# Attention and two feed-forward layers on one core: three experts' weights split straight into their place

## The chip, the cores and the metric

One Trainium2 chip, of which the kernel uses one core. The metric is device time in microseconds (us) of one execution. The engines are named as in the profile: PE is TensorE's matmul and PEld its weight load, DVE is VectorE, ACT is ScalarE, POOL is GpSimd, SP is SyncE, which issues nearly all transfers. POOL issues the gathers and the scattered stores of rows.

## The reference

```python
def _attn_ref(q, k, v, i_gate, f_gate, o_gate):      # B=4, H=8, S=768, D=40
    for t in range(S):
        m_new = np.maximum(f_gate[:, :, t] + m, i_gate[:, :, t])
        ...
        C = f_stab[:, :, None, None] * C + i_stab[:, :, None, None] * np.einsum('bhd,bhe->bhde', vt, kt)
        n = f_stab[:, :, None] * n + i_stab[:, :, None] * kt
        y[:, :, t] = o * h_tilde / denom

def _moe_ref(x, w_in, w_out, alpha):                 # 3072 tokens, 320 -> 2048 -> 320
    h = x @ w_in
    g = np.maximum(h, 0.0) + alpha * np.minimum(h, 0.0)
    return (g @ w_out).astype(np.float32)

def _moe2_ref(x, w_gate, w_output_gate, w1, w2):     # 8 experts, 320 -> 1024 -> 320
    e_idx = np.argmax(x @ w_gate, axis=1)
    ...
    for e in range(E):
        mask = e_idx == e
        h = np.maximum(x[mask] @ w1[e], 0.0)
        out[mask] = gate_w[mask, None] * eom[mask, e, None] * (h @ w2[e])
```

A gated recurrent attention feeds a dense layer, whose result picks one of eight experts for each token. Every expert's two matrices are needed, and which token goes to which expert is known only when the dense layer is through.

## The kernel before

**Stages.** The attention runs in 24 units of 128 positions (4 batches of 6). Three units make a block of 384 tokens, so the dense layer has 8 blocks. In a block it goes through the 2048 inner columns in 16 chunks of 128: `ffn1` (code F) makes a chunk in 8 matmuls, `ffn_split` (g) splits it into a rounded part and a remainder, `ffn2` (S) adds it into the block's output in 9 matmuls. `block_out` and `block_out2` (bo, bp) take a block's output, choose the expert of every token and store the rows to `x1d` in memory. Behind the last block the tokens are sorted by expert (`route_a` to `route_d`, `route_bh`), and 28 to 32 slots of 128 tokens, each of one expert, go through that expert's matrices: slot 0 by `first_rows`, `first_x`, `first_1`, `first_t`, `first_2`, the others in the loop `slots`.

**Split numbers.** A product in nearly full precision is made of products of two rounded parts, so a weight matrix is needed as a high part and a remainder (hi and lo): an ACT copy rounds, and DVE or POOL subtracts. The dense layer's weights come as 64-bit words and are put together on DVE first (`dec_wi`, `dec_wo`).

**The ring.** `ring` is one tile of 33,792 columns, place for the hi and lo parts of three experts (11,264 columns each, RC). While the dense layer runs, the same columns hold its own split weights (16 chunks of wi and wo), the split q and k of the attention (qh, kh), the transposed input of a block (xt_even, xt_odd), the split chunks (gsp) and a pair of tiles for splitting (ehs). They are handed out in that order by `carve`.

**The experts' weights.** Each expert's matrices are cut into 8 pieces (four of 768 columns, four of 640), so there are 64. All through the dense layer a piece is loaded into a staging tile (`expert_load`, el), split (`expert_split`, es: ACT copy, then POOL or DVE) and stored, hi and lo, to a scratch area `scr` in memory (`expert_store`, et). In the last block, as the columns of `ring` come free from the left, `early_load` (ld) reads the first three experts back from `scr` in 33 loads of 1024 columns. The experts behind them are loaded in the slot loop by `next_load`, when the place of one that is done comes free.

**What sets the order.** One list, ORDER, holds the codes of all steps in the order in which they are written out; the table OTHER says for each step whether it takes its usual engine or the other one. Each engine runs its own instructions strictly in that order. The staging tiles (tag raw) are three; the 64-bit words, the experts' pieces and, in `route_c`, the table `a1` share them. `warm` is a matmul on a part of `ring` that was set to zero; its result isn't used.

The split of an expert's piece before (lines 1097 and 1098 of the profile):

```python
A.activation(eh[:, :n], st[:, :n], AF.Copy)
engine(G, V, "expert_split", x).tensor_tensor(st[:, :n].bitcast(F32R), st[:, :n], eh[:, :n].bitcast(F32), ALU.subtract)
```

Other lines that are spoken of: L837 F's matmuls, L845 and L846 the two steps of its activation (ACT, DVE), L852 and L853 its split (ACT, DVE), L865 to L868 S's matmuls, L642 and L650 the products with the gate columns (`gate_w`, `gate_w2`: pw, pwg), L714 the scores of the attention (ps), L971 `route_bh`, L1043 `a1`, L1055 its product (ptok), L331 the gathers of a slot's rows (xg), L1154 `warm`.

## Time and profile before

| | |
|---|---|
| three timed executions, us | 806.36, 809.18, 810.07 (median 809.18) |
| the profiled execution, us | 803.76 |
| its span, first to last instruction, us | 801.7 |
| mean granted TensorE clock, share of full | 0.971 |
| busy: PE, DVE, ACT, POOL | 96%, 58%, 50%, 31% of the span |

The time of an execution holds about 2 us that lie outside the span. The profile's rows come from the one profiled execution, which was shorter than the three timed ones. Busy times of one engine's neighbours overlap a little, since an instruction starts before the one ahead has wholly left the engine.

### The profile page before, as it was taken

How to read it: one execution, taken by the hardware profiler on the slowest of the kernel's cores; microseconds unless marked ns; L12 is line 12 of the kernel's file. 1: busy time of each engine (PE TensorE's matmuls, PEld its weight loads, DVE VectorE, ACT ScalarE, POOL GpSimd, SP SyncE). 2: the span in 40 equal slices, each digit the busy share in tenths (PEclk: the TensorE clock that was granted, in tenths of full speed). 3: DMA queues.
4: the chain of work that ended last, by engine and by line, in shares of the span. 5: the costliest groups of instructions: out<-in, count | busy, mean ns of one | idle time of the engine just before them, and what ended most of it. 6: DMA issues, size and time to landing. Idle time of an engine off the chain costs nothing.

```text
span 801.7 us, 15145 instructions
## 1 busy us (share of the span) xinstructions
PE 766.3 (96%) x4823; PEld 728.3 (91%) x4823; DVE 468.6 (58%) x1143; ACT 400.3 (50%) x846; POOL 252.0 (31%) x266
## 2 busy tenths in 40 slices
PE   3999999999999999999999999986999999999995
PEld 2888999999999999999999999985799999989994
DVE  6757999777666777666677766855323223223231
ACT  3624667647766578567467574332323333233231
POOL 1311323231655443536234432112223222222221
PEclk9857999999999999999999999999999999999998
DMA  7835678988899989998999888989746744661000
GB/s 226 254 130 165 221 244 247 278 252 275 249 306 315 304 285 284 279 285 310 291 292 278 297 271 274 327 295 301 260 169 227 298 161 179 266 249 43 31 20 13
DMA packets 84272, 189.45 MB, mean 236 GB/s; under 512 B 8786, under 2 KB 39567, under 8 KB 82914
## 3 DMA queue, kind: packets, MB, share of 16 engines
q1 hardware_dynamic: 80802, 179.74, 68.8%
q0 software_dynamic: 3392, 8.71, 3.2%
q8 instruction: 44, 0.72, 0.4%
q14 instruction: 34, 0.28, 0.1%
HBM read 267.71 MB, written 55.59 MB: 403 GB/s over the span
## 4 chain that ended last, share of the span: by engine, by line
PE 85%; DMA 6%; issue 3%; ACT 3%; DVE 2%; POOL 1%; POOLq 0%; SPq 0%; ACTq 0%; DVEq 0%
PE ph L837 20%; PE p L293 12%; PE po L293 11%; PE acc L865 7%; PE acc L866 6%; PE acc L868 6%; PE pa L781 5%; PE ps L714 4%; PE p L375 3%; PE pb L730 2%; PE pd L753 2%; PE pwg L650 2%; PE warm L1154 2%; DMA scr<-ring 1%; PE xt L341 1%
## 5 line engine op out<-in xcount | busy, mean ns | idle before, releaser
L837 PE MATMUL ph<-ring 128*128 128x384 f32 x1024 | 198.8, 342 | 0.4 <-DVE ring L853 0.3
L837 PEld LDWEIGHTS ph<-ring 128*128 128x128 f32 x1024 | 176.6, 188 | 2.4 <-DVE ring L853 1.9
L865 PE MATMUL acc<-ring 128*128 128x336 f32 x384 | 123.4, 327 | 0.7 <-ACT ring L852 0.4
L866 PE MATMUL acc<-ring 128*128 128x336 f32 x384 | 120.0, 318 | 0.0
L846 DVE SCALAR_TENSOR_TENSOR ph<-v,al,ph 128x384 f32<-128x384 f32 x128 | 78.1, 618 | 53.9 <-ACT v L845 53.1
L845 ACT ACTIVATE v<-ph 128x384 f32<-128x384 f32 x128 | 61.7, 488 | 80.4 <-PE ph L837 80.2
L293 PE MATMUL po<-ring,hh 128*128 (+1 forms) x448 | 99.3, 308 | 1.0 <-DMA ring<-scr 1.0
L397 DVE TENSOR_SCALAR yo<-po,xg 128x320 f32<-128x320 f32 x27 | 14.9, 551 | 143.9 <-PE po L293 143.9
L293 PE MATMUL p<-ring,xh 128*128 (+1 forms) x336 | 94.4, 402 | 0.6 <-ACT xh L344 0.6
L1098 POOL TENSOR_TENSOR er<-er,ring 128x768 fp32r<-128x768 f32 (+1 forms) x38 | 65.9, 1739 | 82.1 <-ACT ring L1097 81.9
L853 DVE TENSOR_TENSOR ring<-ph,ring 128x384 fp32r<-128x384 f32 x128 | 70.6, 554 | 25.9 <-ACT ring L852 23.0
L852 ACT ACTIVATE ring<-ph 128x384 fp32r<-128x384 f32 x128 | 62.0, 488 | 40.6 <-DVE ph L846 35.7
L398 POOL DMA_INDIRECT out_dram<-yo,tok x28 | 28.4, 1016 | 169.3 <-DVE yo L397 161.5
L868 PE MATMUL acc<-ring 128*128 128x336 f32 x384 | 80.4, 318 | 0.0
L293 PEld LDWEIGHTS po<-ring,hh 128*128 128x128 f32 x448 | 75.8, 187 | 3.9 <-ACT hr L364 1.4
L378 ACT ACTIVATE hh<-p 128x512 fp32r<-128x512 f32 x56 | 30.6, 598 | 93.4 <-PE p L375 93.4
L865 PEld LDWEIGHTS acc<-ring 128*128 128x128 f32 x384 | 73.0, 190 | 1.6 <-ACT ring L852 0.7
L293 PEld LDWEIGHTS p<-ring,xh 128*128 128x128 f32 x336 | 61.6, 190 | 13.2 <-ACT xh L344 0.8
L866 PEld LDWEIGHTS acc<-ring 128*128 128x128 f32 x384 | 72.7, 189 | 0.1
L293 PE MATMUL po<-ring,hl 128*128 (+1 forms) x224 | 69.0, 308 | 0.2 <-DVE hl L379 0.2
L364 ACT ACTIVATE hr<-p 128x512 f32<-128x512 f32 x56 | 33.4, 597 | 69.8 <-PE p L293 69.8
L868 PEld LDWEIGHTS acc<-ring 128*128 128x128 f32 x384 | 64.0, 190 | 0.0
(193 smaller groups left out, 1275.4 us busy)
## 6 DMA issues: line engine op xcount, KB each, us to landing
ring<-scr SPq DMA_DIRECT2D x28, 3072.0 KB
ring<-scr SPq DMA_DIRECT2D x28, 2560.0 KB
ring<-scr SPq DMA_DIRECT2D x33, 512.0 KB
D<-gd SPq DMA_DIRECT2D x48, 256.0 KB
er<-in_ew_dram SPq DMA_DIRECT2D x32, 384.0 KB
scr<-ring SPq DMA_DIRECT2D x32, 384.0 KB
scr<-er SPq DMA_DIRECT2D x32, 384.0 KB
er<-in_ew_dram SPq DMA_DIRECT2D x32, 320.0 KB
```

The source lines that it names most:

```text
L293: mm = T.matmul(o_, lhsT, r, start=start, stop=stop)
L364: A.activation(hr[:, hf * 512 : (hf + 1) * 512], ph, AF.Relu)
L781: T.matmul(pa[:, h * 41 : (h + 1) * 41], t["D", h // 4][:, h % 4], v1[:, h * 41 : (h + 1) * 41], start=True, stop=True,)
L837: T.matmul(ph[:, :384], wi_[i][lo][:, wc], xTs[n % 2][:, xc], start=(a == 0), stop=(a == len(PASSES) - 1),)
L845: A.activation(v, ph[:, :384], AF.Relu, scale=-1.0)
L846: V.scalar_tensor_tensor(ph[:, :384], v, al1[:, i : i + 1], ph[:, :384], ALU.mult, ALU.add)
L852: A.activation(gh, v, AF.Copy)
L853: V.tensor_tensor(gl, v, gh.bitcast(F32), ALU.subtract)
L865: T.matmul(ac, gh[:, sl], hi, start=(i == 0), stop=False)
L866: T.matmul(ac, gh[:, sl], lo, start=False, stop=False)
L868: T.matmul(accs[n][t][:, :NO], gl[:, t * P : (t + 1) * P], hi, start=False, stop=(i == NFC - 1))
L1098: engine(G, V, "expert_split", x).tensor_tensor(st[:, :n].bitcast(F32R), st[:, :n], eh[:, :n].bitcast(F32), ALU.subtract)
```

## The change

The first three experts (24 of the 64 pieces) no longer go through the scratch area. `expert_load`, `expert_split` and `expert_store` run for the other 40 pieces alone, and `early_load` is gone. In its place `held_load` (hl) loads such a piece from the input into a staging tile, and `held_split` (hs) writes its two parts straight into their columns of `ring`: an ACT copy (hi) and a subtraction that always runs on DVE (lo). Three of the loads are issued ahead, the others between the steps of the last block and of slot 0. In `ring` qh now lies ahead of the last chunk of wi, and kh and xt_even near the end. ORDER and OTHER are new as a whole, and `warm` is there 13 times instead of 32.

```diff
-FIRST = 1024
+HELD = 3
...
     "expert_split": (
-        2, 3, 4, 6, 7, 9, 16, 19, 21, 22, 25, 26, 27, 29, 31, 36, 37, 38, 41, 44, 48, 52, 53, 57, 61,
-        63,
+        2, 3, 4, 6, 7, 9, 16, 19, 21, 22, 25, 26, 28, 29, 31, 33, 38, 40, 42, 45, 48, 53, 54, 57, 58,
+        59, 62, 63,
     ),
...
-    "warm": ("warm", zip(range(32))),
-    "el": ("expert_load", zip(range(64))),
+    "warm": ("warm", zip(range(13))),
+    "el": ("expert_load", zip(range(HELD * NPIECE, E * NPIECE))),
...
-    "ld": ("early_load", zip(range(33))),
+    "hl": ("held_load", zip(range(HELD * NPIECE))),
+    "hs": ("held_split", zip(range(HELD * NPIECE))),
...
-    def early_load(p_):
-        c0, c1 = p_ * FIRST, (p_ + 1) * FIRST
...
-            nc.sync.dma_start(ring[:, c0:c].bitcast(F32), scr[e, :, c0 - e * RC : c - e * RC])
...
-        qh = carve(H, P, rows=KR)
-        kh = carve(H, P, rows=KR)
-        xt_even = carve(5, 384)
         wi_, wo_ = [], []
-        for _ in range(NFC):
+        for i in range(NFC):
+            if i == NFC - 1:
+                qh = carve(H, P, rows=KR)
             wi_.append((carve(3, P), carve(3, P)))
...
         gsp = [(carve(384), carve(384)) for _ in range(3)]
+        kh = carve(H, P, rows=KR)
+        xt_even = carve(5, 384)
         ehs = [carve(PC) for _ in range(2)]
...
+        def held_load(x):
...
+            st = stp.tile([P, RW], F32, tag="raw", bufs=3, name=f"eh_{x}")
+            nc.sync.dma_start(st[:, :n], ew[e, :, c0 : c0 + n])
...
+        def held_split(x):
...
+            o = e * RC + base
+            hi, lo = ring[:, o : o + n], ring[:, o + half : o + half + n]
+            A.activation(hi, st, AF.Copy)
+            engine(V, G, "held_split", x).tensor_tensor(lo, st, hi.bitcast(F32), ALU.subtract)
```

In the diff's code V is DVE, G POOL and A ACT; held_split has no entry in OTHER, so its second step takes the usual engine, V. Lines behind the ones that are gone have moved up by 8 (L837 is now L829), those behind the new functions down by 10.

Three places of the new order. First PE in the first third of the start, where the attention of units 1 and 2 and the gate products wait for their inputs. Before:

```order
L781 MATMUL pa_408<-kv_1_208,D_1_325 128x41 x4
L822 MATMUL pt_424<-cst,y_389 128x128 x3
L1154 MATMUL warm_436<-ring 128x512
L1154 MATMUL warm_438<-ring 128x512
L1154 MATMUL warm_440<-ring 128x512
L1154 MATMUL warm_442<-ring 128x512
L650 MATMUL pwg_455<-wgt,woT_237 128x16 x3
L642 MATMUL pw_461<-cst,f_wo_343 128x128 x3
L1154 MATMUL warm_472<-ring 128x512
L1154 MATMUL warm_474<-ring 128x512
L714 MATMUL ps_0_483<-q_2_433,k_2_431 128x128 x4
```

The same place now:

```order
L773 MATMUL pa_414<-kv_1_317,D_1_271 128x41 x4
L634 MATMUL pw_433<-cst,f_wo_335 128x128 x3
L814 MATMUL pt_439<-cst,y_403 128x128 x3
L706 MATMUL ps_0_452<-q_2_358,k_2_446 128x128 x4
L1164 MATMUL warm_458<-ring 128x512
L706 MATMUL ps_1_474<-q_2_358,k_2_446 128x128 x4
```

Between the second half of unit 1's product with v (pa) and unit 2's scores (ps) six warm matmuls and one gate product (pwg) are gone. Counted up to the first F, PE's row holds 31 warm matmuls before and 13 now, 9 and 8 pw, 8 and 6 pwg, and the same steps of units 0 to 2.

Second ACT at the end of the last block, around the split of its chunks 14 and 15 (ph is a chunk, v its activation, xr a row tile of the block's output). Before:

```order
L852 ACTIVATE ring<-ph_6145 128x384
L344 ACTIVATE xh_6178<-xt_6174 128x384
L845 ACTIVATE v_6193<-ph_6184 128x384
L852 ACTIVATE ring<-ph_6184 128x384
L880 ACTIVATE xr_0_6218<-acc_0_5791 128x320
```

Now:

```order
L1092 ACTIVATE ring<-eh_5988 128x640
L844 ACTIVATE ring<-ph_5954 128x384
L837 ACTIVATE v_6033<-ph_6024 128x384
L1092 ACTIVATE ring<-eh_5994 128x640
L844 ACTIVATE ring<-ph_6024 128x384
L1092 ACTIVATE ring<-eh_6049 128x640
L1092 ACTIVATE ring<-eh_6053 128x640
L872 ACTIVATE xr_0_6076<-acc_0_5600 128x320
```

The copy of piece 13 (eh_5994) now stands ahead of the split of the last chunk (ph_6024); it writes columns of chunk 14, so it waits for that chunk's S. Slot 0's xh, which stood ahead of the last chunk, comes later.

Third DVE behind the last block, from the reciprocals of `block_out2` (xr) to the ranks of `route_c` (rb). Before:

```order
L912 TENSOR_TENSOR sm_6252<-sm_6252,zs_6256 128x3
L914 RECIPROCAL xr_0_6218<-sm_6252 128x4
L914 RECIPROCAL xr_1_6222<-sm_6252 128x4
L914 RECIPROCAL xr_2_6226<-sm_6252 128x4
L1025 TENSOR_TENSOR rb<-ranks,oh_all 128x24
```

Now:

```order
L906 RECIPROCAL xr_2_6084<-sm_6099 128x4
L1093 TENSOR_TENSOR ring<-eh_6060,ring 128x768
L1093 TENSOR_TENSOR ring<-eh_6062,ring 128x768
L336 TENSOR_TENSOR xl_6124<-xt_6119,xh_6123 128x256
L337 TENSOR_TENSOR xh_6123<-xt_6119,xh_6123 64x128
L1093 TENSOR_TENSOR ring<-eh_6073,ring 128x768
L1017 TENSOR_TENSOR rb<-ranks,oh_all 128x24
```

Three held pieces and slot 0's remainders now stand ahead of `route_c`. Behind `a1` two more pieces stand ahead of the token lists, and three more behind slot 0's splits; `route_d` follows these, ahead of slot 1's remainders.

## Rows read from the trace of the kernel before

**Rows 1.** The page: part 1 (busy time of each engine, its share of the span, instructions) and, of part 2, the granted clock of TensorE in 40 slices of 20 us.

```profile
PE 766.3 (96%) x4823; PEld 728.3 (91%) x4823; DVE 468.6 (58%) x1143; ACT 400.3 (50%) x846; POOL 252.0 (31%) x266
...
PEclk9857999999999999999999999999999999999998
```

**Rows 2.** Busy time by stretches of the span: us of the stretch, then for each engine busy us and (x) instructions, the granted clock, the DMA share and GB/s.

```profile
0.00:20.00 20.00, 6.77 (x25) 4.87 (x25) 12.66 (x39) 6.30 (x14) 2.16 (x7) 1.00 0.74 226
20.00:60.00 40.00, 39.03 (x170) 34.16 (x169) 27.34 (x70) 18.18 (x45) 10.90 (x14) 0.69 0.62 193
...
100.00:200.00 100.00, 99.91 (x682) 98.10 (x682) 80.72 (x191) 62.11 (x135) 29.59 (x34) 0.98 0.83 259
...
400.00:500.00 100.00, 99.31 (x651) 97.69 (x650) 71.00 (x171) 63.98 (x133) 40.10 (x38) 1.00 0.88 282
500.00:540.00 40.00, 37.85 (x251) 37.44 (x250) 26.87 (x79) 14.04 (x30) 5.32 (x10) 1.00 0.92 317
540.00:560.00 20.00, 14.93 (x100) 12.63 (x98) 11.14 (x57) 5.00 (x11) 4.15 (x8) 0.91 0.86 284
560.00:580.00 20.00, 17.59 (x97) 14.90 (x98) 6.37 (x14) 6.69 (x13) 4.95 (x5) 1.00 0.76 285
```

**Rows 3.** The same view in stretches of 4 us, around the first product of the dense layer.

```profile
36.00:40.00 4.00, 4.00 (x18) 3.51 (x18) 2.77 (x6) 0.84 (x1) 1.98 (x3) 0.50 0.87 263
...
64.00:68.00 4.00, 4.00 (x15) 3.19 (x15) 2.69 (x9) 1.41 (x3) 0.00 (x0) 0.50 0.40 129
68.00:72.00 4.00, 4.00 (x28) 3.43 (x26) 2.59 (x10) 2.54 (x7) 0.24 (x1) 0.79 0.79 242
72.00:76.00 4.00, 4.00 (x23) 3.45 (x23) 3.92 (x12) 2.74 (x9) 1.39 (x2) 1.00 0.87 263
```

**Rows 4.** The timeline of PE, in order of time, at the start: start us, us, engine, line, operation, out<-in, count, and in brackets the idle time before it and what ended it.

```profile
22.61 3.78 PE L714 MATMUL ps<-q,k 40*128 40x128 f32 x16
...
33.70 2.11 PE L714 MATMUL ps<-q,k 40*128 40x128 f32 x16
...
41.77 2.05 PE L1154 MATMUL warm<-ring 128*128 128x512 f32 x4
43.63 1.29 PE L650 MATMUL pwg<-wgt,woT 128*128 128x16 f32 x6
44.76 0.88 PE L642 MATMUL pw<-cst,f_wo 128*128 128x128 f32 x3
...
73.73 3.05 PE L837 MATMUL ph<-ring 128*128 128x384 f32 x16
...
105.18 1.41 PE L650 MATMUL pwg<-wgt,woT 128*128 128x16 f32 x12
```

**Rows 5.** Groups of instructions by line with their shapes: busy us and mean ns of one, idle us before them and what ended it.

```profile
L846 DVE SCALAR_TENSOR_TENSOR ph<-v,al,ph 128x384 f32<-128x384 f32 x128 | 78.1, 618 | 53.9 <-ACT v L845 53.1
...
L853 DVE TENSOR_TENSOR ring<-ph,ring 128x384 fp32r<-128x384 f32 x128 | 70.6, 554 | 25.9 <-ACT ring L852 23.0 <-PE pd L753 0.6 <-PE ps L714 0.6
...
L1097 ACT ACTIVATE ring<-er 128x768 fp32r<-128x768 f32 x32 | 26.8, 840 | 7.6 <-DMA er<-in_ew_dram 5.1 <-DMA scr<-ring 2.4
...
L1098 DVE TENSOR_TENSOR er<-er,ring 128x640 fp32r<-128x640 f32 x15 | 13.0, 880 | 0.7 <-ACT ring L1097 0.4
...
L1098 DVE TENSOR_TENSOR er<-er,ring 128x768 fp32r<-128x768 f32 x11 | 11.1, 1005 | 3.1 <-ACT ring L1097 2.8
...
L971 DVE TENSOR_SCALAR bh<-cst,rb 128x128 f16<-128x128 f32 x24 | 6.8, 342 | 0.0
```

**Rows 6.** The timeline of PE at the end of the last block and behind it.

```profile
531.50 0.31 PE L865 MATMUL acc<-ring 128*128 128x336 f32 x1
...
532.88 1.55 PE L837 MATMUL ph<-ring 128*128 128x384 f32 x8
534.27 0.32 PE L865 MATMUL acc<-ring 128*128 128x336 f32 x1
...
537.98 0.52 PE L341 MATMUL xt<-cst,x 128*128 128x128 f32 x3 [2.15 <-DMA x<-x1d,tok]
...
541.73 0.42 PE L865 MATMUL acc<-ring 128*128 128x336 f32 x1 [0.43 <-ACT ring L852]
...
561.79 0.55 PE L341 MATMUL xt<-cst,xg 128*128 128x128 f32 x3 [1.80 <-DMA xg<-x1d,tok]
```

**Rows 7.** The timelines of SyncE's queue and of ScalarE: one load of an expert's piece from its issue to the first instruction that reads it.

```profile
508.23 0.81 SPq L1089 DMA_DIRECT2D er<-in_ew_dram  x1
...
511.61 0.74 ACT L1097 ACTIVATE ring<-er 128x640 fp32r<-128x640 f32 x1 [1.10 <-DMA er<-in_ew_dram]
```

**Rows 8.** The timeline of VectorE from the end of the last block to the token lists of the slots.

```profile
543.11 0.49 DVE L879 COPY lg<-acc 128x16 f32<-128x16 f32 x3 [0.85 <-PE acc L868]
...
546.98 0.15 DVE L1025 TENSOR_TENSOR rb<-ranks,oh_all 128x24 f32<-128x24 f32 x1
...
549.48 0.95 DVE L1043 TENSOR_TENSOR a<-cst,rb 128x768 f16<-128x768 f32 x1
...
553.11 0.19 DVE L995 TENSOR_TENSOR tok<-rb 128x31 int32<-128x31 f32 x1
```

**Rows 9.** The chain of waits that ended last: start us, us, what. Two transfers behind the last block.

```profile
547.84 7.21 DMA x1d<-xr
...
555.93 5.81 DMA xg<-x1d,tok
```

More of the change, by code (lines that the diff above doesn't have):

```diff
@@ L122 @@
-g F route_a route_first et et S ld g F bh bh bh S g S S ld ld ld bh bh bh el bh bh F g S ld ld bh el bh bh bh bh
-bh es F F g g S S F ld es ad ld ld ld g F S S bh bh ld ld g first_set bp F F g S g ld bh bh ld bh S bh bh ld F g
-route_first2 F g ld S S F g ld ld S ld first_rows first_x F ld g S S bo route_b ld ld ld ld ld bp route_c
-route_d et ld ld first_1 route_c2 first_t first_1 first_t first_2 first_2 first_2 first_2 et ld ld
+ah gates_d lo do load_gates pq load_cst lo load_gates load_wg lo do do gates gates_e lk lv do gw so lo gates lq
@@ new lines @@
+lq do do gates_e gw do do load_sel do so gates_d so do pq pq li gw pt gv do di di di do so set_al1 ad gv si gv
+load_g ae load_g ae load_g log li load_g load_g li di as as ae gw ae lg lg di di di di di lv pt si si ab lo do
+sg ah do lk pq ay ae warm load_gates lq li do di ad di di ay si as el as warm warm load_g lv ay warm ay pq warm
+lo do do ab ae so lo gw ac lk ay ay ay as warm es et do do ay lo do as ah gv lq gates gw ac ab ay so do so do ay
+gv gv gw ay ay do warm warm warm warm warm warm lq li di lk gates_e di do pt di gates_d si lv pk ac so lo lg pq
@@ new lines @@
+pq load_g load_g load_g do do ae ad li do pt warm gw di F pk ae F ah gv so di lo g g pk di as as si li di log gw
+lo do do lk do load_g di di lg F gv F gv gw si S S lv g do g do do so ae ae ab ad li di di di S lg lo so lg gw
+do lo as pk pk si do gv log do F load_g pq li do do do gv ae F lq as so g ay ay S lv so gw gw di di di g pt li
+li S lk ay di sg pt ay di ah si di di di si F ab as load_g di lk ae load_g S ad si g F load_g as g li di gv di
+li di di di F di el es F lk g load_g si lv S ac S li di ah si ae di di pk g li di F et di ay di si ay ay ay ab g
@@ new lines @@
+ay ah ay ay ae ae es et S S F F g g as pk S ac ae F g pq ab ay ay ay ay F S F S g g as S as F g ac ab ay ay ay
+ay F F S g ac S g F F S g S S g F g F S g S bo F F S g g hl route_a route_first F bh bh F S g S S hs hs g F hs
+hl hl bh bh S S g bh bh bh bh hs F hs bh F g bh g S bh hl hs S hl hl bp F F bh bh g hs g bh hs S S bh bh bh F bh
+bh bh hl hl F hl S g hs hs g bh S hs F F g S S hl hl hs hs hl route_first2 g F S hs g hl hs hl hs first_rows hl
+hl S hl bo bp hs hs first_x route_b hs hl hl route_c hs hs first_1 hl route_c2 hl first_1 first_t first_t
@@ L126 @@
+first_2 first_2 hs hs hl hs first_2 first_2 route_d
 """
@@ L160 @@
     "set_al1": ("set_al1", [()]),
[L161 to L162 removed]
+    "warm": ("warm", zip(range(13))),
+    "el": ("expert_load", zip(range(HELD * NPIECE, E * NPIECE))),
     "ac": ("att_c", zip(range(24))),
[L164 to L165 removed]
+    "es": ("expert_split", zip(range(HELD * NPIECE, E * NPIECE))),
+    "et": ("expert_store", zip(range(HELD * NPIECE, E * NPIECE))),
     "pk": ("prep_k", zip(range(24))),
@@ L1083, in mlstm_moe_kernel @@
         pieces = {}
+        def held_load(x):
+            e, p_ = divmod(x, NPIECE)
+            c0, n, base, half = PIECES[p_]
+            st = stp.tile([P, RW], F32, tag="raw", bufs=3, name=f"eh_{x}")
+            nc.sync.dma_start(st[:, :n], ew[e, :, c0 : c0 + n])
+            pieces[x] = st
+        def held_split(x):
+            e, p_ = divmod(x, NPIECE)
+            c0, n, base, half = PIECES[p_]
+            st = pieces.pop(x)[:, :n]
+            o = e * RC + base
+            hi, lo = ring[:, o : o + n], ring[:, o + half : o + half + n]
+            A.activation(hi, st, AF.Copy)
+            engine(V, G, "held_split", x).tensor_tensor(lo, st, hi.bitcast(F32), ALU.subtract)
         def expert_load(x):
```

73 lines of the change are left out of this document (26 added, 47 removed).

## The prediction

> **What bounds the kernel now.** I read the page first. PE is busy 766.3 of 801.7 us, DVE 58%, ACT 50%, POOL 31% [rows 1]. So a transfer or a split on another engine is worth something only where PE waits, or where it runs at its lower clock. The view by stretches says where that is: from 100 to 200 us PE is busy 99.91, from 400 to 500 us 99.31 of 100 us [rows 2]. The waits lie at the two ends. In the first 20 us PE is busy 6.77, and then 37.85 of 40 from 500 to 540, 14.93 of 20 from 540 to 560, 17.59 of 20 from 560 to 580 [rows 2]. The granted clock stands at 9 and 8 tenths in the first two slices of 20 us, at 5 and 7 in the third and fourth, and at 9 (which is 90% or more) behind these [rows 1]. In stretches of 4 us it is 0.50, the lower of the two levels (1.2 of 2.4 GHz), from 36 to 68 us, 0.79 from 68 to 72, and 1.00 behind that, with PE busy 4.00 of 4.00 in all of them that are shown [rows 3]. The timeline of PE gives both prices: 16 products ps take 2.11 us at the full clock and 3.78 at the lower one, and six products pwg (L650) take 1.13 us (43.63 to 44.76) there [rows 4].
>
> From this: the 24 pieces that are no longer split, stored and read back in the first seven blocks free ACT, POOL, DVE and the transfers in stretches where PE has no wait to lose. I cost that at nothing. What remains are the start, the last block and what lies behind it.
>
> **The start.** Ahead of the first F (73.73 [rows 4]) PE's row has 18 warm matmuls fewer, two pwg and one pw fewer. Four warms take 1.86 us at the lower clock (41.77 to 43.63 [rows 4]), 0.465 each, so 18 take 8.4 us at most; some of before's stood in the stretch at 1.00 and take half. The gate products aren't gone but moved behind the first F: two pwg at 1.13 and a pw at 0.7 (estimated from its 0.88, overlap taken off) are 3 us, and half of that behind F (twelve pwg take 1.41 there [rows 4]). So 1.5 us are won. The largest gain is 9.9 us.
>
> Against it: a warm matmul costs its time only where PE would have had other work. From 20 to 60 us PE is idle for 1 us only [rows 2], but warms stand in that sum, and one that covered a wait for ACT or DVE gives the wait back when it goes. DVE has 40 us of work in the first 60 (12.66 and 27.34), ACT 24.5 (6.30 and 18.18) [rows 2], so neither is a bound as a sum; what can be late is the chain of small steps from one unit to the next, which no row separates. Then the clock: after the 16 ps at 33.70 at full pace [rows 4] it falls, and a shorter start may meet the lower level sooner or leave it later. Bounds: -9.9 and 0. I take the middle, -5, since neither end has a row that is nearer; the first F would then stand near 68 us.
>
> The Trainium skill ("TensorE: Matmul & The Clock Gate", Part 1: The HAM clock gate) speaks against this part: it says that the throttled state is the default and that activity releases it, so that matmuls taken out of the start would be missed. The trace agrees only in part, as the clock does rise by 72 us, but PE was busy 4.00 of 4.00 from 36 to 40 and from 64 to 68 with 0.50 granted [rows 3], warms among its work. What that rule would do here is the third rival.
>
> **The last block.** PE needs 1.39 us for an F or S of one chunk: acc at 531.50, ph at 532.88, acc at 534.27 [rows 6]. From the first S behind which a held piece stands (chunk 4 of the block) to the end these are 10 F and 12 S, 30.6 us, some 31 with the small products. In the same stretch of the new order DVE has 10 activations at 0.61 (78.1 over 128), 11 remainders at 0.55, 16 held remainders (eight of 768 columns at 1.0, eight of 640 at 0.87), 19 bh at 0.28 (6.8 over 24) [rows 5] and about a dozen small steps of block_out2, 2 us by estimate: 6.1 + 6.1 + 15.0 + 5.3 + 2 = 34.5. The last two held pieces (1.7) stand behind the last g. So 32.8 us must be through before the last S can begin, against PE's 31: DVE becomes about as long as PE, and a little longer. At the very end piece 13 waits for the S of chunk 14 and stands ahead of the last chunk's split on both engines: copy 0.74 (the ACT line of [rows 7]), remainder 0.55 and a copy of g, about 2.1 us, where PE waited 0.43 before (541.73 [rows 6]). What goes: PE's wait of 2.15 us for x of slot 0 (537.98 [rows 6]), as first_x now stands behind the last S. Added up: 1.8 + 1.7 of waits and 0.3 of held pieces ahead of lg, less 2.15 saved, +1.7. I take +2; the bounds are 0 (DVE works ahead, and only the saved wait and the last one count) and +5 (no overlap of these waits, and the copies on ACT late as well).
>
> Can the loads keep up? A load took 3.4 us from issue to its first reader (508.23 to 511.61 [rows 7]), its two steps some 1.8 us [rows 5]; with three staging tiles that is 5.2 us for three, 1.75 a piece, and 13 pieces behind the three loaded ahead need 23 of 31 us. The cover is there as long as a load lasts under some 5 us.
>
> **Behind the last block.** lg is read at 543.11, `route_c` begins at 546.98, a1 at 549.48 takes 0.95, the token lists are there at 553.11 [rows 8]. Three held remainders of 768 columns (3 x 1.0 [rows 5]) now stand ahead of `route_c`, two more (1.9) between a1 and the lists, three (2.6) and `route_d` ahead of slot 1's remainders. POOL waits for the lists to issue slot 1's gather, and PE for that: it waited 1.80 us at 561.79 [rows 6]. The five that stand ahead of the lists would cost 4.9 us if DVE had no gaps there, but the store of x1d, which the gather needs too, takes 7.21 us and the gather 5.81 [rows 9], with 285 GB/s under way beside them [rows 2], of which the read of the ring is gone. If those two shrink, they give back some of it. What the slots read in the end: at best the gather is 1 us earlier (both transfers shorter, DVE in gaps), at worst 4 us later. I take +2.7, as the three pieces ahead of `route_c` are on the path for certain. The slot loop is unchanged and PE-bound, so an early or late start moves its end by as much.
>
> **Sum.** -5 + 2 + 2.7 = -0.3 on the profiled execution's 803.76 (span 801.7 and 2 us outside), 803.5. That execution was 5.4 us below the median of the timed ones, 809.18, and I forecast against the median: 809. About 0.5%, 4 us, is what a measurement of this kernel can tell from no change.
>
> **Rivals.** First, faster: the warms were pure ballast. For it: no engine but PE has a sum near the bound from 20 to 60 us, and 30 us at half the clock make each of them dear. The start then gives 8 to 9.9, and in the end stage the shorter transfers and the 2.15 us cover most of the held pieces, leaving +1 to +2: 809.2 - 9 + 1.5 = 802. Against it: warms that cover waits.
>
> Second, slower: DVE is the engine that sets the end. The held remainders take turns with g in a strict order, so a late piece holds the next chunk's split, and PE cannot run ahead beyond its few chunk buffers. It decides from the point where DVE needs more than 2.78 us for each chunk (an F and an S): 34.5 us over 11 chunks is 3.1. Price: +5 in the block, +4 behind it, and the start gives only 3 because its waits come back: 809.2 + 6 = 815. For it: the sums above. Against it: DVE may start on these pieces before PE's stretch begins.
>
> Third, slower by the clock: the lower level holds until about as much work behind the first F as now ahead of it. Price from ps: one us of work at full clock costs 3.78 / 2.11 = 1.8 there. If the clock comes up 8 us behind the first F, 4 or 5 us of work take 8, and the start's gain of 5 is gone: 809.2 + 4.7 = 814. The rule of the Trainium skill that activity releases the throttle (the section named above) would give this one. Against it: the level was left at 70 us with no more PE activity in the rows than before.
>
> **How the numbers follow.** Forecast (both ends cancel) 0.39, with its own range of 805 to 813; first rival 0.34; second 0.19; third 0.08. The range runs from 800.5 (the first rival with nothing given back) to 817 (the second with its full price). Faster: the first rival and a little of the forecast, 0.36. Within 0.5%: most of the forecast and the edges of the rivals, 0.37. Slower: 0.27.
>
> **What would show it.** The first ph on PE before 70 us: the start as forecast; at 64 to 66 the first rival; at 72 or later no gain. Granted clock below 1.00 behind the first F: the third. In the last block, PE's idle time in front of S put down to ACT or DVE (ring), in sum over 5 us, with DVE near 100% from 510 to 545: the second. a1 about 3 us further behind lg than the 6.4 of now (543.11 to 549.48), slot 1's xt further behind lg than the 18.7 of now (561.79): the tail. I am wrong if PE shows new waits in the blocks between 100 and 500 us, or if the slots' loads find the transfers in another state.

## The result and the profile after

Timed 20 times each, the changed kernel takes 815.75 us (809.0 to 823.96) and the kernel before 807.96 us (800.84 to 815.6): a ratio of 1.0106, with a 95% interval of 1.008 to 1.0132. It is slower by 8 us, where 809 and no change were forecast. The profiled execution has a span of 810.3 us (812.02 in all) against 801.7.

The page of the changed kernel, PE's line and the granted clock, beside [rows 1]:

```profile
PE 768.8 (95%) x4804; PEld 731.6 (90%) x4804; DVE 482.3 (60%) x1158; ACT 396.4 (49%) x844; POOL 226.9 (28%) x251
...
PEclk9999999998999999999999999997999999999998
```

PE is busy 2.5 us longer than before, and idle 41.5 us instead of 35.4. Busy time by stretch (us of the stretch, then PE, PEld, DVE, ACT and POOL busy, granted clock, DMA share, GB/s), beside [rows 2]:

```profile
100.00:200.00 100.00, 96.86 (x645) 94.07 (x644) 74.96 (x182) 61.53 (x135) 34.08 (x36) 0.97 0.75 242
400.00:500.00 100.00, 99.54 (x652) 98.55 (x651) 68.78 (x161) 54.20 (x116) 16.66 (x24) 1.00 0.39 114
500.00:540.00 40.00, 40.00 (x243) 39.32 (x242) 34.57 (x91) 21.63 (x43) 0.71 (x3) 1.00 0.34 98
```

From 100 to 200 us PE was busy 99.91 before; it is 96.86 now, at a granted clock of 0.97. That stretch lies in the first seven blocks of the dense layer, where the prediction put the cost at nothing. From 400 to 500 us nothing is lost (99.54, and 99.31 before), and from 500 to 540 PE is busy 40.00 us (37.85 before).

The timeline of PE at the start, beside [rows 4]:

```profile
23.87 3.78 PE L706 MATMUL ps<-q,k 40*128 40x128 f32 x16
...
34.77 3.78 PE L706 MATMUL ps<-q,k 40*128 40x128 f32 x16
...
68.84 4.26 PE L829 MATMUL ph<-ring 128*128 128x384 f32 x16
```

The first F begins at 68.84 instead of 73.73. Sixteen ps take 3.78 us twice, against 2.11 at the faster pace [rows 4]; that is the pace of the lower clock, although the record of this execution grants 1.00 there. The first two F take 4.26 us instead of 3.05, so by their durations the lower level reaches into them. The first S comes at 81.00 us, and before at 79.39: in the new order more steps of the attention and the gates stand between the first F and the first S.

The timeline of PE at the end of the last block and behind it, beside [rows 6]:

```profile
547.05 0.43 PE L857 MATMUL acc<-ring 128*128 128x336 f32 x1 [0.44 <-ACT ring L844]
...
568.92 0.49 PE L332 MATMUL xt<-cst,xg 128*128 128x128 f32 x3
570.98 1.16 PE L284 MATMUL p<-ring,xh 128*128 x3 [1.57 <-DVE nsl_i L1073]
```

The last S begins at 547.05 (541.73 before) and waits 0.44 for its split, as before (0.43). The three stages follow from these starts alone: start to first F -4.9; first F to last S 478.2 us instead of 468.0, +10.2; last S to the end of the span 263.2 instead of 260.0, +3.2. The sum is +8.5, the difference of the spans.

The timeline of DVE behind the last block, beside [rows 8]:

```profile
549.38 0.33 DVE L871 COPY lg<-acc 128x16 f32<-128x16 f32 x3
...
552.73 1.80 DVE L1093 TENSOR_TENSOR ring<-eh,ring 128x768 fp32r<-128x768 f32 x2
...
555.20 0.96 DVE L1093 TENSOR_TENSOR ring<-eh,ring 128x768 fp32r<-128x768 f32 x1
...
558.72 0.95 DVE L1035 TENSOR_TENSOR a<-cst,rb 128x768 f16<-128x768 f32 x1
559.59 1.68 DVE L1093 TENSOR_TENSOR ring<-eh,ring 128x768 fp32r<-128x768 f32 x2
...
561.62 0.19 DVE L987 TENSOR_TENSOR tok<-rb 128x31 int32<-128x31 f32 x1
...
566.33 2.30 DVE L1093 TENSOR_TENSOR ring<-eh,ring 128x640 fp32r<-128x640 f32 x3
...
570.81 0.13 DVE L1073 CAST nsl_i<-rb 1x1 int32<-1x1 f32 x1
```

From lg to a1 it is 9.3 us now and 6.4 before; three held pieces stand between (552.73 and 555.20). Three more (566.33) and `route_d` stand ahead of slot 1, whose first product waits 1.57 us for the last value of `route_d` (570.81).

The place of the loss shows best in one stretch, 155 to 500 us, before and after:

```profile
155.00:500.00 345.00, 343.92 (x2272) 340.06 (x2271) 240.68 (x563) 225.19 (x468) 146.61 (x141) 1.00 0.92 285
```

```profile
155.00:500.00 345.00, 338.56 (x2226) 333.99 (x2225) 234.21 (x545) 208.78 (x445) 121.21 (x123) 0.99 0.70 217
```

PE has 1.1 us of idle time there before and 6.4 us after. The longest waits of PE from 100 to 500 us in the changed kernel (who waits for whom: us in total, times, longest):

```profile
PE pd L745 <- POOL kt L672: 2.1, 1, 2.1
PE ph L829 <- DVE ring L845: 1.4, 1, 1.4
PE pd L745 <- ACT v L837: 1.1, 1, 1.1
PE acc L860 <- DVE ring L845: 0.9, 2, 0.7
```

Before, the longest were 0.4 us for kt and 0.3 us at two other places.

### The profile page after: what moved, and what is told of

Its sections match the earlier page's. It is cut to its first block, busy times and chain, and to the rows that moved or that the text cites. A ratio compares the mean times of both kernels' runs of the same rounds, so it can differ in the third digit from the quotient of the medians.

```text
span 810.3 us, 14909 instructions
## 1 busy us (share of the span) xinstructions
PE 768.8 (95%) x4804; PEld 731.6 (90%) x4804; DVE 482.3 (60%) x1158; ACT 396.4 (49%) x844; POOL 226.9 (28%) x251
## 4 chain that ended last, share of the span: by engine, by line
PE 68%; DMA 13%; DVE 8%; ACT 5%; issue 2%; SPq 1%; POOL 1%; POOLq 0%; ACTq 0%; DVEq 0%
PE ph L829 15%; PE p L284 11%; PE po L284 10%; PE acc L860 5%; PE acc L857 5%; PE acc L858 5%; PE ps L706 4%; DMA ring<-scr 4%; PE pa L773 4%; DMA scr<-er 3%; PE p L366 3%; DMA k<-in_ks_dram 2%; PE pd L745 1%; PE pwg L642 1%; PE pb L722 1%
## 5 line engine op out<-in xcount | busy, mean ns | idle before, releaser
L829 PE MATMUL ph<-ring 128*128 128x384 f32 x1024 | 202.4, 345 | 1.4 <-DVE ring L845 1.4
L829 PEld LDWEIGHTS ph<-ring 128*128 128x128 f32 x1024 | 179.1, 191 | 3.0 <-DVE ring L845 2.5
L837 ACT ACTIVATE v<-ph 128x384 f32<-128x384 f32 x128 | 61.9, 487 | 91.1 <-PE ph L829 90.1
L284 PE MATMUL p<-ring,xh 128*128 (+1 forms) x336 | 96.1, 407 | 3.6 <-ACT xh L335 2.0
L694 ACT ACTIVATE D<-D,EKT 128x128 f32<-128x128 f32 x192 | 60.1, 393 | 2.5 <-DMA D<-gd 2.4
```

The source lines that it names most:

```text
L284: mm = T.matmul(o_, lhsT, r, start=start, stop=stop)
L694: A.activation(d[:, j], d[:, j], AF.Exp, bias=EKT[:, c, i + j : i + j + 1])
L829: T.matmul(ph[:, :384], wi_[i][lo][:, wc], xTs[n % 2][:, xc], start=(a == 0), stop=(a == len(PASSES) - 1),)
L837: A.activation(v, ph[:, :384], AF.Relu, scale=-1.0)
```

## The experiments

There are eighteen runs: aft2 and aft3 are the changed kernel again, and h1b is h1 again. All but aft2, a single execution, were timed in turn with the kernel before. "Ratio" is against that kernel, with its 95% interval; differences of medians between kernels that were not measured side by side are rougher. Starts of an S are read from PE's timeline, nine products to a chunk; all 1,152 stand in every trace. Chunks are counted from 0 through all eight blocks, so chunk 16 is the first of the second block, 112 the first of the last and 127 its last. A profile is one execution.

**Is the work that was taken away worth nothing? (b40, b8, a8)** b40 is the kernel before with 40 of its 64 pieces; the codes of the others are taken out of ORDER.

```diff
-    "el": ("expert_load", zip(range(64))),
+    "el": ("expert_load", zip(range(24, 64))),
...
-            nc.sync.dma_start(ring[:, c0:c].bitcast(F32), scr[e, :, c0 - e * RC : c - e * RC])
+            nc.sync.dma_start(ring[:, c0:c].bitcast(F32), scr[e + 3, :, c0 - e * RC : c - e * RC])
```

> The kernel before with only 40 of the 64 pieces loaded, split and stored, in its first 40 places of the order; the reads of the last block stay, from the areas of experts 3 to 5 (the values of the first three experts are left out). Theory 1 (what the change lost lies in the new order of blocks 1 to 6, where PE now waits 6.6 us between 100 and 400 us against 0.3 before): the work taken away was hidden, so the time is that of before, 808 us, within 3 us, and PE waits under 1.5 us from 100 to 400. Rival (less work in the middle is itself worth something or costs something there, because the transfers or POOL are near a bound): over 4 us away from 808.

Measured: 803.76 us, ratio 0.9922 (0.9886 to 0.9958). The removed work is worth 3.5 us by the medians and 6 by the ratio: not nothing, though PE waited only 1.1 us from 155 to 500 us, the middle.

b8 goes on to 8 pieces, and a8 does the same with the changed kernel. Of b8's edit:

```diff
-    "el": ("expert_load", zip(range(64))),
+    "el": ("expert_load", zip(range(8))),
...
-            scr[ds(eo, 1), :, c0:c1].rearrange("o p c -> (o p) c"),
+            scr[0, :, c0:c1],
```

> The kernel before without 56 of the 64 pieces (only expert 0's eight are loaded, split and stored, and all reads take that expert's area; the values of the others are left out), order otherwise the same: the partner of the run a8. If pieces are hidden in the order of before: within 2 us of b40's 803.8. If every piece costs something there too: 3.5 us per 24 pieces by b40, so some 5 us less, 799. Against a8 (804.5) it shows what the new start and end are worth without pieces: by the terms of the prediction, -3 to -5 and +2.4.

> The changed kernel without 32 of its 40 pieces that go through memory (only expert 3's eight are loaded, split and stored; all later slots read that expert's weights), same order otherwise. Theory 1 in its stronger form (the waits in blocks 1 to 6 come from these pieces, whose transfers and splits stand ahead of the attention's and F's steps in the queues): PE waits under 2 us from 100 to 400 instead of 6.6, no clock drop there, 806 us, 803 to 809. Rival (the waits come from the order of the attention and F steps themselves): waits stay, 812 or more.

Measured: b8 800.65 us, ratio 0.9943 (0.9915 to 0.9972); a8 804.54 us, ratio 0.9957 (0.9926 to 0.9989). With 8 pieces the changed order has no wait left in the middle:

```profile
155.00:500.00 345.00, 345.00 (x2302) 343.59 (x2302) 228.19 (x558) 193.21 (x426) 89.54 (x107) 1.00 0.44 117
```

The 32 pieces that a8 leaves out cost the changed kernel 11 us by the medians and 12 by the ratios. In the old order the same number of pieces, from b40 to b8, cost 3 us by the medians and nothing by the ratios, whose intervals overlap. So it is not the amount of work but where the new order puts it. As for what -3 to -5 and +2.4 had been expected to give, the ratios of a8 and b8 overlap: without the pieces, the new start and end together show neither a gain nor a loss. In the two profiles a8 reaches the S of chunk 109 some 3 us earlier (484.6 and 487.6) and takes 2.7 us longer from there (314.7 and 312.0).

**The new place in the old order (h1, h1b, h3), and the old middle behind the new start (h2).** h1 is the changed kernel with another list of steps: before's up to the S of chunk 109, with the 40 pieces in its first 40 places, then the new one's remaining steps. Its table OTHER is before's too, with the pieces' entries moved along, and it has all 32 warm matmuls.

```diff
     "prep_kt": (
-        0, 2, 3, 4, 8, 9, 10, 12, 13, 15, 18, 19, 20, 21,
+        2, 6, 8, 10, 12, 13, 14, 15, 16, 18, 19, 21, 22,
...
 ORDER = """
-ah gates_d lo do load_gates pq load_cst lo load_gates load_wg lo do do gates gates_e lk lv do gw so lo gates lq
...
+warm gates_d pk lo do do do load_gates load_gates load_cst li load_sel lv gates lo so di lq load_wg load_g
...
```

> The changed kernel (new place, no store and second read for three experts, its layout), but in the order of the kernel before up to the S of chunk 109, with the 40 pieces in that order's first 40 places, and in the new order from there. Theory 1: start and middle as before, so first F at 73 to 74 us, PE waits under 1.5 us from 100 to 400, and the end stage about 1 us shorter than before (what the two profiles show between chunk 116 and the end): 807 us, 804 to 809. Rival 2 (the loss lies in the new place itself: DVE and ACT in the last block, or the layout): as slow as the changed kernel, 814 to 817.

> h1 once more, side by side with the changed kernel. Theory (the order of start and middle costs, the new place does not): 804 to 806 where before has 807, and 8 to 10 us under the changed kernel of the same call. Rival (h1's first figure was chance): 808 or more, within 6 us of the changed kernel.

Measured: h1 806.13 us, 0.9966 (0.9929 to 1.0004); again, side by side with the changed kernel, 807.32 us, 0.9988 (0.9956 to 1.002), where the changed kernel took 815.32. The same place on chip, the same layout and the same tail as in the changed kernel, with the old order ahead, is as fast as the kernel before. Its middle (155 to 500 us):

```profile
155.00:500.00 345.00, 343.03 (x2282) 339.60 (x2282) 237.42 (x561) 212.26 (x450) 120.89 (x127) 1.00 0.72 220
```

Where the loss lies can be read at the S of chunk 109. Every kernel with the old or the new order has the same 2,999 products of PE ahead of it, warm ones left out. It starts in the kernel before, the changed kernel and h1, in this order, at

```profile
489.76 0.40 PE L865 MATMUL acc<-ring 128*128 128x336 f32 x1
```

```profile
497.21 0.32 PE L857 MATMUL acc<-ring 128*128 128x336 f32 x1
```

```profile
492.06 0.40 PE L857 MATMUL acc<-ring 128*128 128x336 f32 x1
```

In seven profiles with the old order ahead (the kernel before, bw, h1, h1b, h3, t1, t2) it lies between 486.0 and 492.1 us, in the three of the changed kernel at 497.2, 501.4 and 498.4, 9.6 us later in the mean. From there to the end it is 313.1, 312.9 and 311.6 us in the changed kernel, 312.0 in the kernel before, 313.2 and 312.9 in h1 and h1b.

So the loss of 8 us against the kernel before comes with the new order of start and middle, together with the table OTHER, which was not tested apart from it. The new place, with the work that it saves, comes out even. That the end stage takes back what b40 gains would fit, but isn't shown.

h3 is h1 with its seam at chunk 112:

> h1 with the seam at the S of chunk 112 instead of 109, so that the order of before goes on for three chunks more. Theory: the wait of 1.26 us at 496 us goes, and the new place with the old start and middle is some 4 us faster than before: 804, 801 to 806. Rival: the seam's wait moves, as h1, 806.

Measured: 810.95 us, 1.0044 (1.0014 to 1.0075), slower than h1. The wait at the seam was 2.61 us instead of 1.26, and from the last S to the end it took 5 us longer than in h1 (266.9 and 261.7); why is not known. A seam three chunks further on changes more than the wait that it was to remove; the expectation missed that.

h2 has the new start up to the S of chunk 5, then the old order to chunk 109:

> As h1, but with the new order's start up to the S of chunk 5, then the order of before to the S of chunk 109, then the new order. Theory 1: the start's gain stays (first F at 69 us, some 3 us of it left after the low clock) and the middle loses nothing: 803.5 us, 801 to 807, faster than before and some 12 us under the changed kernel. Rival 2: 811 or more. Rival 3 (the early start only moves the waits into the next stage): as h1.

Measured: 812.34 us, 1.0051 (1.002 to 1.0081), 6 us slower than h1, with its first F at 67.2 us instead of 75.7. The lead over h1 was 2.8 us at the S of chunk 16 and gone by chunk 104. The seam costs something itself (a wait of 1.84 us at 117 us and a lower clock behind it), so h2 doesn't price the start cleanly; its early first F at least gave no gain. In the two profiles h2 stands where h1 does at the S of chunk 109 (492.2 and 492.1 us), so with the old middle the new start loses nothing up to there. What h2 loses against h1 in them comes behind the last S (264.8 and 261.7 us to the end), where both have the same steps; this stays unexplained.

**The warm matmuls (bw, w6).** bw leaves 18 of the 32 out of the kernel before, w6 puts 8 more behind the first F of the changed one.

```diff
-    "warm": ("warm", zip(range(32))),
+    "warm": ("warm", zip(range(14))),
```

> The kernel before without 18 of its 32 warm matmuls (the 6th to the 23rd, which stood from 41.8 to 68 us at the lower clock), nothing else. If they were ballast, as the prediction's first rival has it: first F at 65 to 66 us and 799 to 801. If they only filled waits: first F at 71 to 73, 805 to 807. If they bring the clock up: the lower clock lasts beyond the first F by several us, 808 or more.

Measured: 807.37 us, 1.0008 (0.9974 to 1.0042). In the profile the first F came at 70.8 instead of 73.7 us, the S of chunk 16 1.5 us earlier, and by chunk 104 nothing of that was left. 18 warm matmuls, 8.4 us by their rows, are worth nothing in the time, to within 3 us: they filled waits, as the second of the expectations has it.

```diff
-pq load_g load_g load_g do do ae ad li do pt warm gw di F pk ae F ah gv so di lo g g pk di as as si li di log gw
...
+pq pq load_g load_g load_g do do ae ad li do pt warm gw di F pk ae F ah gv so di lo g g pk di as warm as warm
...
```

> The changed kernel with 8 warm matmuls more, spread behind the first F up to the S of chunk 6 (75 to 105 us), 1.7 us of PE work at the full clock. If the lower clock behind the early first F is chance that PE's work there decides: less of it, 813 or less, and 1.00 granted from 76 to 110 us. If warms don't matter: 817.

Measured: 814.14 us, 1.0096 (1.006 to 1.0132), as the changed kernel. Warm matmuls there show no effect, and the granted clock still fell to 0.64 from 80 to 84 us.

**How regular is it? (aft2, aft3)** The changed kernel twice more, unchanged.

> The changed kernel once more, for a second profile. Theory 1b: the waits of the first profile come again at the same places (kt near 193 us, F near 316 us, S near 353 us), since they are set by the order. Rival (chance in the transfers): other places, and a sum of PE waits from 100 to 500 us that differs by more than half from 7.4.

> The changed kernel once more: 815 (1.0106 of before) by the earlier runs; PE's work between the S of chunk 16 and of chunk 112 some 5 us longer than before's 345.4 in its profile, the end of the last block 1 to 2 us shorter, the tail 3 us longer. If the start's gain survives, the S of chunk 16 at 153; if the clock falls behind the first F, at 158 to 162.

Measured: aft2 816.03 us; aft3 815.32 us, 1.0106 (1.0071 to 1.0142). The waits for kt and of F near 317 us came in all three profiles, at the same steps (sums from 100 to 500 us of 6 to 8 us). But the start differs. The first two F of aft2, and its stretches behind them:

```profile
72.43 3.04 PE L830 MATMUL ph<-ring 128*128 128x384 f32 x16
```

```profile
76.00:80.00 4.00, 4.00 (x31) 3.85 (x30) 3.83 (x9) 2.21 (x7) 1.55 (x2) 0.90 0.61 217
80.00:84.00 4.00, 4.00 (x17) 4.00 (x16) 3.90 (x10) 0.80 (x3) 0.00 (x0) 0.50 0.85 211
84.00:88.00 4.00, 4.00 (x24) 4.00 (x23) 0.82 (x4) 1.90 (x6) 0.25 (x1) 0.75 1.01 335
```

PE is recorded as busy without a gap, and the granted clock falls to the lower level from about 79 to 86 us, after two F at the full pace; it falls again from 96 to 103. The S of chunk 16 came at 161.8 us there, against 153.2 in both the others. With the old start it lies between 150.5 and 160.3 us (seven profiles: the kernel before, b8, h1, h1b, h3, t1, t2; mean 155.0), with the new start between 150.2 and 161.8 (nine: the changed kernel's three, a8, e3, u1, k1, k2, t3; mean 154.1). The start's gain is about 1 us in the mean, and the scatter from one execution to the next is several times that. The first F scatters as much: 68.8 to 75.7 us in these seven, 65.8 to 72.4 in these nine. Nor does a lead last: h1 and h1b are one kernel, with the S of chunk 16 at 160.3 and 150.5 us and the S of chunk 109 at 492.1 and 489.5.

**What makes PE wait in the middle (e3, u1, k1, k2).** The chain of waits of the changed kernel around 193 us, where PE waits longest (start us, us, what):

```profile
177.16 7.25 DMA scr<-er
...
184.43 0.33 SPq L1099
...
184.85 4.26 DMA scr<-ring
...
189.21 0.85 ACT ring L1107
...
190.14 2.29 POOL er L1108
192.43 0.69 POOL kt L672
...
193.16 0.91 PE pd L745 x6
```

A store out of a staging tile takes 7.25 us; only then may SyncE issue the next load (184.43), a store of high parts stands behind that load (184.85), ACT's copy waits for it, POOL's remainder for the copy, and kt stands behind the remainder on POOL. The clock then:

```profile
190.00:200.00 10.00, 7.44 (x36) 7.00 (x35) 6.72 (x17) 6.13 (x10) 6.59 (x4) 0.72 0.99 348
```

0.72 over 10 us is 2.8 us of work lost beside the wait: the fall comes behind it, when PE is busy again. e3 gives the copies a third tile for the high parts:

```diff
-        ehs = [carve(PC) for _ in range(2)]
+        ehs = [carve(PC) for _ in range(3)]
...
-            eh = ehs[x % 2]
+            eh = ehs[x % 3]
```

> The changed kernel with three tiles for the high parts of pieces instead of two (ring had 1024 columns left), so that a piece's copy on ACT no longer waits for the store of the piece two before it; order unchanged. Theory 1b: the chain at 177 to 193 us (two stores, then the copy, POOL's remainder, kt, PE's wait of 2.05 us and a lower clock behind it) goes, 811, 808 to 813.5. Rival (the copies wait for their loads anyway): 815, as the changed kernel.

Measured: 810.55 us, 1.0056 (1.0023 to 1.0089). The median is 5 us lower, as expected (its interval still overlaps that of the changed kernel a little), but not in the way expected: the wait for kt was still there (1.86 us). If looser buffers help, then at no single place that this profile names.

u1 spreads the pieces evenly:

```diff
-load_g et lk S el el F ae ah ae as F S S g g es as et pk es lq ay F ay et sg F ac g S S g pt ad el es pq et ab
...
+load_g lk S F ae ah ae as es F el S S et g g as pk lq ay F ay sg F es el ac g S S g pt et ad pq ab ay ay F F es
...
```

> The changed kernel with nothing moved but 35 of its 40 pieces' loads, splits and stores (and the first two loads ahead for the held pieces, which now follow the last store): between F 18 and F 100 they stand in an even beat of 8.9 us of PE work, each split 8 us behind its load and each store 4 us behind its split. Theory 1b (the new order packs the pieces so that copies, POOL and SyncE wait for buffers and transfers with the attention's steps behind them): PE waits between 100 and 500 us fall from 7.4 to under 2.5 us and the time to 806, 803 to 809. Rival (40 pieces cost the same wherever they stand, because transfers are near a bound): 813 or more.

Measured: 831.18 us, 1.0294 (1.023 to 1.0358), the largest miss here, 25 us above the expectation. The middle, and the largest of its waits (us in total, times, longest):

```profile
155.00:500.00 345.00, 328.99 (x2124) 324.41 (x2123) 224.09 (x525) 203.46 (x433) 120.05 (x122) 0.97 0.71 218
```

```profile
PE ph L828 <- DVE ring L844: 8.2, 5, 2.6
```

So an even beat is no cure, and in this form the theory of packing fell. What the runs support is narrower: waits that come with the order and go when the pieces go (a8). That a piece is cheap or dear by the step that stands behind it on ACT, DVE or POOL fits the chain above, but is shown for that one chain alone.

k1 moves only unit 9's kt ahead of two pieces' splits, and k2 adds e3's tile:

```diff
-load_g et lk S el el F ae ah ae as F S S g g es as et pk es lq ay F ay et sg F ac g S S g pt ad el es pq et ab
...
+load_g load_g et lk S el el F ae ah ae as F S S g g pt es as et pk es lq ay F ay et sg F ac g S S g ad el es pq
...
```

> The changed kernel with one step moved: unit 9's prep_kt (the product kt on POOL) now stands ahead of the splits of pieces 33 and 34 instead of behind them. Theory (the wait of PE for kt at 193 us, 2.05 us, and the granted clock of 0.72 and 0.94 in the 20 us behind it, 3.4 us of work at half speed, are one mechanism): both go, 810.5, 808 to 813. Rival (the wait only moves to the next late step, or the clock falls anyway): 814 or more.

> k1 with three tiles for the high parts (e3). If e3's gain (5 us) and k1's are two things: 806, 803 to 808. If e3 gained by the same wait: as k1 or e3, 810.

Measured: k1 811.15 us, 1.0073 (1.0041 to 1.0104); k2 812.17 us, 1.0047 (1.0009 to 1.0084). The wait for kt went, and another came at the same moment, 193 us, for DVE behind the output of the attention:

```profile
PE pa L772 <- DVE ring L817: 2.8, 1, 2.8
```

The clock fell behind it as well (0.66 in that stretch). k1's interval overlaps the changed kernel's, so a gain is not shown. So two steps at least were late there together, and freeing one uncovered the next.

**The tail (t1, t2, t3).** t1 is h1 with fewer pieces ahead of the token lists and three remainders on POOL; t2 adds the third tile; t3 is the changed kernel with both.

```diff
-hl hs first_rows hl hl S hl bo bp hs hs first_x route_b hs hl hl route_c hs hs first_1 hl route_c2 hl first_1
-first_t first_t first_2 first_2 hs hs hl hs first_2 first_2 route_d
+hl hs first_rows hl hl S hl bo bp first_x route_b hs route_c hs hl first_1 route_c2 hs hl hl first_1 first_t
+first_t route_d first_2 first_2 hs hl hs hl first_2 first_2 hs hs hs
...
+    "held_split": (
+        16, 17, 18,
+    ),
```

> h1 with another tail: the token sort's last part and route_d now stand ahead of most of the pieces that are left behind the last block (before route_c one held piece instead of three, between a1 and the token lists none instead of two, route_d ahead of the last five pieces), and the remainders of pieces 16 to 18 run on POOL. Theory (the tail's loss of 2.7 us is these pieces on DVE ahead of a1, the lists and route_d): from the last S to slot 1's first product 20.5 to 21.5 us instead of 23.0, and 803.5 in all, 801 to 806. Rival (the transfers x1d and xg or the pieces' loads set it): as h1, 806.

> t1 with three tiles for the high parts of pieces. If copies on ACT also wait for these stores in the order of before: some 2 us less than t1, 801.5. If not (h1 shows PE waits of 2.5 us only between 100 and 500): as t1.

> e3 (the changed kernel with three tiles for high parts) with the tail of t1. Theory: 2.5 us under e3's 810.5, 808; it tells the tail's term apart in the new order, where start and middle are as changed. Rival: as e3.

Measured: t1 808.53 us, 1.0026 (0.9993 to 1.0058); t2 809.48 us, 1.0038 (1.0009 to 1.0067); t3 813.30 us, 1.0078 (1.0043 to 1.0114). By the medians t1 is 2.4 us slower than h1 and t3 2.7 slower than e3, with intervals that overlap: the gain that was expected is not there, and t2 shows none for the third tile in the old order. In the profiles the way from the last S to the end is longer with the new tail, 266.6 us in t1 against 261.7 in h1 and 268.0 in t3 against 263.6 in e3. POOL and DVE in t1's tail:

```profile
543.58 3.59 POOL L1096 TENSOR_TENSOR ring<-eh,ring 128x768 fp32r<-128x768 f32 x2 [1.98 <-ACT ring L1095]
548.30 1.80 POOL L1096 TENSOR_TENSOR ring<-eh,ring 128x768 fp32r<-128x768 f32 x1 [1.13 <-ACT ring L1095]
```

```profile
544.21 1.21 DVE L1023 TENSOR_SCALAR rb<-rb 128x8 int32<-128x8 int32 x1
...
545.46 1.74 DVE L1025 TENSOR_SCALAR rb<-rb 128x8 f32<-128x8 int32 x1
...
548.43 1.75 DVE L966 TENSOR_SCALAR bh<-cst,rb 128x128 f16<-128x128 f32 x1
...
561.26 2.40 DVE L1096 TENSOR_TENSOR ring<-eh,ring 128x768 fp32r<-128x768 f32 x3
```

Three DVE steps take 1.21, 1.74 and 1.75 us, each until the remainder that runs on POOL ends; in h1, where POOL is idle there, the last two are these, with a third step between them:

```profile
553.49 0.17 DVE L1022 TENSOR_SCALAR rb<-rb 128x8 f32<-128x8 int32 x1
...
554.10 0.36 DVE L1028 TENSOR_TENSOR rb<-oh_all,rb 128x192 f32<-128x192 f32 x1
554.38 0.34 DVE L963 TENSOR_SCALAR bh<-cst,rb 128x128 f16<-128x128 f32 x1
```

That is some 4 us on the way to a1, and the three remainders that were moved off DVE had taken 2.9 there. From lg to a1 it is 10.6 us in t1 and 9.7 in h1, from lg to the token lists 13.0 and 12.6. So the larger part of the 4.9 us lies behind the lists. Slot 1's first product starts 24.0 us behind the last S (23.0 in h1), and its third waits for DVE, where three of the pieces left for later (561.26) stand ahead of slot 1's remainders:

```profile
564.36 0.79 PE L287 MATMUL p<-ring,xh 128*128 x1 [2.24 <-DVE xh L340]
```

What is left of the 4.9 us was not traced to a step.

## Why the prediction was wrong

By its own steps, with the starts read from PE's timeline (the kernel before: S of chunk 16 at 155.6 us, 344.5 us from there to chunk 112, 41.6 to chunk 127, 260.0 to the end; the three profiles of the changed kernel: 153.2, 161.8 and 153.2; 353.8, 349.5 and 355.0; 40.0 to 40.1; 263.2, 263.0 and 261.8):

- "I cost that at nothing", of the pieces taken out of the first seven blocks and of the order there: **this step failed**, by 5 to 10 us, 8.2 in the mean (the old order in other profiles, with 40 pieces or with all: 343.1 to 350.3, the longest behind the earliest start). The argument was that PE had no wait to lose in the middle. That bounds a gain (and even the gain was not nothing: b40). It says nothing about a loss. The new order is a new order of the middle too, with other steps behind the pieces' copies and splits, and PE's 1.1 us of idle time became 6.4, with a lower clock behind the longest wait. h1 and h1b show it: the old order and table with the new place have none of the loss, and a8 shows that it goes when the pieces go. The rows that were shown of the new order were all from the start and the end.
- The start, -5: the first F came 4.9 us earlier, as forecast, but one execution could not show that: in other profiles it starts at 68.8 with the old order (h1b) and at 72.4 with the new one (aft2). The gain of the start is about 1 us in the mean of the profiles, within their scatter and near the other bound that was given (0). The middle between two bounds had no row behind it. Three things go with the smaller value: the lower clock reaches into the first F or returns behind it, gate products moved behind F cost their time there, and in bw 18 warm matmuls filled waits. So the first rival (warms are ballast) is out. Of the third rival (a late clock) aft2 shows the effect, where 161.8 - 153.2 makes 8.6 us of difference at chunk 16, but not each execution does. The price of the lower clock was taken from 16 ps at 22.61 us [rows 4], where the record grants 1.00; only their duration says that they ran at the lower level.
- The last block, +2: measured -1.6. DVE is indeed about as long as PE at its end; it is busy 9.97 of 10 us from 530 to 540:

```profile
530.00:540.00 10.00, 10.00 (x60) 9.56 (x59) 9.97 (x23) 6.02 (x11) 0.00 (x0) 1.00 0.70 208
```

  But the last S waited 0.44 us where 2.1 had been worked out, and PE has no idle time from 500 to 540. DVE worked ahead, which was the lower bound that the prediction gave (0, with the 2.15 us for x saved beside it), and the stage came out a little below that bound. The second rival, DVE as the engine that sets the end, is out.
- Behind the last block, +2.7: measured +2.7 in the mean of the three profiles, by the steps named: lg to a1 +2.9, and slot 1 behind three pieces and `route_d`, its first product 23.9 us behind the last S instead of 21.2. With the last block that makes +1.1 where +4.7 was forecast.
- In these profiles alone the terms are +0.5 for the start up to chunk 16 (aft2 is one of the three), +8.2, -1.6 and +2.7. They add up to 9.8 us, the difference of the spans. The medians of all executions differ by 7.8; the one profile of the kernel before came from an execution 4 us shorter than its median.

What the trace of after was to show did appear: PE's new waits between 100 and 500 us were named as the sign that the prediction is wrong.

What stays open: which steps of the middle would have to change places, or engines, to bring the changed kernel to a8's level. The waits come back at the same steps in each profile, but k1 and u1 show that neither the removal of one nor an even spread does it. No version that does the whole work was clearly faster than the kernel before; h1 equals it.

## What to carry to other kernels

When a diff brings a new order as a whole, compare it everywhere on the engines that the bound engine waits for, not only at the places that the edit is about; a bound engine with hardly any idle time has little to gain there, but it can lose. Time that is won early is worth its face value only if everything behind it can move up too: here a first F that came 3 us (bw) or 8 us (h2) earlier in its profile was given back within the next 100 chunks. Before work is moved from one vector engine to another, look at what short steps run on the first while the second is busy.

## What the runs showed of the hardware

A remainder (two inputs, 128 x 768) on POOL held some steps of DVE to its end. A step of 8 columns that takes 0.17 us in h1 took 1.74 in t1, and one of 128 columns 1.75 instead of 0.34. This came three times in each of t1, t2 and t3. In t3 one of them is a step with two inputs, 1.97 us instead of the 0.36 of L1028 in h1. POOL and DVE there:

```profile
552.79 1.80 POOL L1095 TENSOR_TENSOR ring<-eh,ring 128x768 fp32r<-128x768 f32 x1 [0.43 <-ACT ring L1094]
```

```profile
552.83 1.97 DVE L1030 TENSOR_TENSOR rb<-oh_all,rb 128x192 f32<-128x192 f32 x1
```

Not every step is held. Four that start beside t1's first remainder, from 543.58 us on, took 0.15 to 0.29 us; three of them read a result of PE, as this one does:

```profile
543.90 0.18 DVE L1020 TENSOR_TENSOR rb<-ranks,oh_all 128x24 f32<-128x24 f32 x1
```

The Trainium skill ("SBUF — State Buffer", SBUF: two separate sides) says that DVE and GpSimd share a pair of ports as an exclusive lock, held for a whole instruction, and that of DVE's steps only those with two inputs from SBUF (the memory of the tiles) or in a mode with two ports take it. The steps that were held to a remainder's end agree with the lock. Which of the short steps ran in such a mode no trace here shows.

The granted clock can fall while PE is recorded as busy all the time (aft2, 79 to 86 us). It fell behind a PE wait of 2.05 us (0.72 from 190 to 200 us in the changed kernel) and stayed at 1.00 behind one of 1.2 us for the same step (aft2, 200 to 210 us). In some executions its record stands at 1.00 through a stretch in which the products take the time of the lower level (the changed kernel's ps at 23.87 and 34.77 us). The durations are the safer sign.
